# Attention scores of the 128-query units: fp32 products replaced by products of rounded halves, with new tiles and a new order of units

## Chip, cores and metric

The kernel runs on one core of one Trainium2 chip. The metric is device time in microseconds (us) of one execution; three runs of the kernel before are shown. A profile is taken of one further execution.

## What is computed

Causal attention for 4 batches, 12 heads, 448 positions and 64 values a head, and then a feed-forward block on the 1792 tokens of 768 values:

```
scores = q @ k.T / 8, masked above the diagonal
attn   = softmax(scores) ;  a = attn @ v
x      = a, heads side by side: 1792 x 768
xn     = x / sqrt(mean(x*x) + 1e-6) * rms_g
out    = (silu(xn @ w_gate) * (xn @ w_val)) @ w_out
```

The weights have 768 x 1536 (gate, value) and 1536 x 768 elements. All results are fp32.

## The kernel before, in words

**Units.** Attention is cut into units of two heads (a chunk of 128 features, `NP` = 6 chunks) and some queries. Kind 0 has the first 256 queries of a batch against 256 keys, kind 1 the next 128 queries against 384 keys, kind 2 the last 64 queries of two batches at once against 448 keys (`QUERIES`, `KEYS`, line 31). Queries and keys lie transposed, 64 rows a head: head 0 in rows 0 to 63, head 1 in rows 64 to 127. `GROUPS` (line 33) puts the units into three groups of tokens: 512 tokens (two batches of kind 0), 512 (the other two), and 768 (kind 1 of four batches, kind 2 of both pairs). `UNITS` (line 35) lists them by group, then by chunk, then by kind and number; 24 units are of kind 1 and 12 of kind 2. The first 24 units of the list are of kind 0.

**A unit's steps.** `steps_s` (line 173) computes scores on TensorE (`scores`, line 183: for kind 1 one fp32 product a head, 64 rows, 128 weights, 384 columns), then VectorE scales, masks and takes the maximum (line 202), ScalarE takes the exponential with its sum (line 205), VectorE the reciprocal (line 214), GpSimd multiplies (line 210; ScalarE in part of the earlier units). `steps_t` (line 234) transposes the probabilities on TensorE in two halves (a head each, line 249) through the one bank `t`, and VectorE (line 253) or ScalarE (line 255) copies them out. `steps_a` (line 259) multiplies by the values (line 275) and copies the result (line 292).

**Order.** Everything is in program order by hand. The feed-forward block of a group runs while the attention of the next group runs: the main loop (line 900) issues a part of six fp32r products of 128 x 512 (`ffn_part`, lines 475 to 477: each factor is a rounded half plus a rest, three products), then as many attention steps as the pace allows, then one tick. `post(delay, f)` issues f at the end of a later tick. In the group of 768 tokens `round_of_two` (line 809) takes two units at a time in four steps, one a tick: the second transpose of unit p + 1 with a visit (scores of p + 3 and p + 4, value products of p and p + 1), then the transposes of p + 2 (two) and p + 3 (one). Even units use the banks x and y for their scores, odd ones the banks s.

**Loads.** All transfers are issued by SP, in order. `load_qk(p + 4)` (line 151) is posted two ticks after the scores of p into one of four buffers of 2 x 512 elements, whatever the kind; `load_v` (line 160) two ticks after a visit for the next two units, into one of three buffers. Between them stand loads of weights (line 400) and stores of sums of weights (line 454). A transfer into a buffer waits for the last reader of what lay there, and all issues behind it wait with it.

**Splitting into halves.** The kernel splits other operands already: the hidden layer with a ScalarE copy (line 503) and a subtraction on VectorE (line 505) or GpSimd; weights likewise (lines 429, 431).

Of the kernel before, what the change touches and what calls it, by code (L numbers as in the profile page):

```python
# [10 lines left out]
F32 = mybir.dt.float32  # L11
F32R = mybir.dt.float32r
# [10 lines left out]
P = 128  # L23
# [4 lines left out]
W = 512  # L28
# [1 line left out]

QUERIES, KEYS, KB, NKB = (256, 128, 128), (256, 384, 448), (128, 128, 112), (2, 3, 4)

GROUPS = (((0, 2, 0, 0),), ((0, 2, 2, 0),), ((1, 4, 0, 0), (2, 2, 0, W)))
NG = len(GROUPS)
UNITS = [(g, kind, c, k, NP * (first + k) + c, base + QUERIES[kind] * k)
         for g, parts in enumerate(GROUPS) for c in range(NP)
         for kind, n, first, base in parts for k in range(n)]
LAST = {(g, c): max(i for i, u in enumerate(UNITS) if u[0] == g and u[2] == c)
        for g in range(NG) for c in range(NP)}
ENDS = [max(i for i, u in enumerate(UNITS) if u[0] == g) + 1 for g in range(NG)]  # L40
MASKED = -8.0e9


T = dict(c0=0, c1=1, c10=5, c2=4, c20=16, c3=4, c30=18, c26=5, c36=5, c5=6, c50=19, c56=7, exp=1, exp0=3, gt=1, hh=1, hl=4, ws=5, ld2=7,
         ld=4, ld1=11, lv=5, norm0=7, norm1=2, r0=1, acc=10, acc4=7, dg=1, spread=2, r1=5, so=3, wl=2, wl0=7, wl2=5, wl4=1, xl=2, xl0=9)
LOAD = (4, 12, 24, 36, 48, 60, 72, 84)
CONVERT = (14, 26, 38, 50, 62, 85, 86)
# [15 lines left out]
def attention_ffn(ctx: ExitStack, tc: tile.TileContext, qk0, qk1, qk2, v, v2, w, g, out, out2):  # L63
# [35 lines left out]
    def f32(ap):  # L99
        return ap.bitcast(F32)  # L100
# [20 lines left out]
    eps = const.tile([P, 1], F32, name="eps")  # L121
    nc.vector.memset(eps, 1e-6)
    tiny = const.tile([P, 1], F32, name="tiny")
    warm_up = const.tile([P, 1], F32, name="warm_up")
    nc.vector.memset(tiny, 1e-9)
    g_sb = const.tile([P, KD], F32, name="g_sb")

# [4 lines left out]
    def post(delay, fn):  # L132
        if delay <= 0:
            fn()
        else:
            later.setdefault(now[0] + delay, []).append(fn)
# [7 lines left out]
    xr, xh, xl, acc, xq = {}, {}, {}, {}, {}  # L144


    raw_qk, raw_v, hs = {}, {}, {}
    nsc = -1.0 / float(D) ** 0.5
    av_ps = bank("a").rearrange("p (s c) -> p s c", s=2)

    def load_qk(p):
        if p < len(UNITS):
            _, kind, _, _, row, _ = UNITS[p]
            raw_qk[p] = raw.tile([P, 2, W], F32, tag="qk", name="qk_r")
            if kind == 2:
                nc.sync.dma_start(out=raw_qk[p], in_=qk2[row])
            else:
                nc.sync.dma_start(out=raw_qk[p][:, 0], in_=(qk0, qk1)[kind][row])

    def load_v(p):  # L160
        if p < len(UNITS):
            _, kind, _, _, row, _ = UNITS[p]
            raw_v[p] = raw.tile([P, 2, 4, 2, D], F32, tag="v", name="v_r", bufs=3)
            if kind == 2:
                nc.sync.dma_start(out=raw_v[p][: KB[2]], in_=v2[row])
            else:
                nc.sync.dma_start(out=raw_v[p][:, 0, : NKB[kind]], in_=v[row, :, : NKB[kind]])

    def blocks(kind):
# [3 lines left out]
    def steps_s(p):  # L173


        if not 0 <= p < len(UNITS):
            return []
        _, kind, _, _, _, _ = UNITS[p]
        pr = hs[p] = dict(norms=[])
        bl = blocks(kind)  # L180
        nb = 2 * len(bl)

        def scores(pss):
            for i, (o, wd) in enumerate(bl):
                for h in range(1 + (kind == 2)):
                    for e in range(2):
                        r = raw_qk[p][e * D: (e + 1) * D, h]
                        if kind == 2:
                            ps, q0, nq = pss[e][h * D: (h + 1) * D, :wd], 0, D
                        else:  # L190
                            ps, q0, nq = pss[e][:, o: o + wd], i * P, P
                        k0 = nq if kind else 2 * P
                        nc.tensor.matmul(ps, r[:, q0: q0 + nq], r[:, k0: k0 + wd],  # L193
                                         start=True, stop=True)

        def softmax(e, i, pss):
            o, wd = bl[i]
            ps, sp = pss[e][:, o: o + wd], pr["sp"][e][:, o: o + wd]
            n = len(bl) * e + i
            nm, sm, rs = (pr[m][:, n: n + 1] for m in ("nm", "sm", "rs"))  # L200
            mk = mask2 if kind == 2 else mask[:, 3 * P - wd:]
            nc.vector.tensor_tensor_reduce(  # L202
                out=sp, in0=ps, in1=mk, scale=nsc, scalar=3.0e38,
                op0=ALU.add, op1=ALU.min, accum_out=nm)
            post(T["exp" if p >= ENDS[0] else "exp0"], lambda: nc.scalar.activation(  # L205
                sp, sp, AF.Exp, bias=nm, scale=-1.0, accum_out=sm))
            if ENDS[0] - 2 <= p < ENDS[1]:
                pr["norms"].append(lambda: nc.scalar.mul(sp, sp, rs))
            else:
                pr["norms"].append(lambda: nc.gpsimd.tensor_scalar(  # L210
                    sp, sp, rs, 1.0, op0=ALU.mult, op1=ALU.mult))

        def norm():
            nc.vector.reciprocal(pr["rs"][:, :nb], pr["sm"][:, :nb])  # L214
            post(2 if ENDS[0] - 2 <= p < ENDS[0] else 0, lambda: [f() for f in pr["norms"]])

        def step():
            for nm in ("nm", "sm", "rs"):
                pr[nm] = st_p.tile([P, 4], F32, tag=nm, name=nm)
            pr["sp"] = [sp_p.tile([P, S], F32, tag="sp", name="sp") for _ in range(2)]  # L220
            pss = [bank(t_) for t_ in "xy"] if p > ENDS[1] + DP and p % 2 == 0 else [
                bank("s", 2) for _ in range(2)]
            scores(pss)
            for e in range(2):
                for i in range(len(bl)):
                    softmax(e, i, pss)
            post(T["exp" if p >= ENDS[0] else "exp0"], lambda: nc.scalar.activation(
                pr["sm"][:, :nb], pr["sm"][:, :nb], AF.Identity, bias=tiny))
            post(T["norm1" if kind else "norm0"], norm)
            post(2, lambda: load_qk(p + 4))  # L230

        return [step]

    def steps_t(p):

        if not 0 <= p < len(UNITS):
            return []
        _, kind, _, _, _, _ = UNITS[p]
        pr = hs[p]
        kb = KB[kind]  # L240

        def some(e):
            pt = pr["pt", e] = pt_p.tile([P, W], F32, tag=f"pt{e}", name="pt")
            ps = bank("x" if e and p < ENDS[1] + 1 else "t")
            at = 0
            for j in range(NKB[kind]):
                for o, wd in blocks(kind):
                    if kb * j < wd:
                        nc.tensor.transpose(ps[:kb, at: at + P],  # L249
                                            pr["sp"][e][:, o + kb * j: o + kb * (j + 1)], ident)  # L250
                        at += P
            if kind or (e and p < ENDS[0]):
                nc.vector.tensor_copy(pt[:kb, :at], ps[:kb, :at])  # L253
            else:
                nc.scalar.copy(pt[:kb, :at], ps[:kb, :at])

        return [lambda e=e: some(e) for e in (0, 1)]

    def steps_a(p):


        if not 0 <= p < len(UNITS):
            return []
        g_, kind, c, k, _, base = UNITS[p]
        pr = hs[p]
        kb, nq = KB[kind], QUERIES[kind]

        def products():
            for h in range(1 + (kind == 2)):
                at = 0  # L270
                for j in range(NKB[kind]):
                    q0, n = ((0, 2 * P), (P, P))[j] if kind == 0 else (D * h, (P, D)[kind - 1])
                    a0 = at + (D * h if kind == 2 else 0)
                    for e in (0, 1):
                        nc.tensor.matmul(  # L275
                            av_ps[e * D: (e + 1) * D, p % 2, q0: q0 + n], raw_v[p][:kb, h, j, e, :],
                            pr["pt", e][:kb, a0: a0 + n], start=(j == 0), stop=(j == NKB[kind] - 1))
                    at += n if kind == 0 else P

        def copy():  # L280
            if g_ == 2 and base == 0:
                if c < 3:
                    xq[c] = w64_p.tile([P, 2, XT], F32, tag="w64", name="xq")
                xr[g_, c] = xq[c % 3][:, c // 3]
            elif base == 0:
                xr[g_, c] = xr_p.tile([P, W], F32, tag="xr", name="xr")
            x = xr[g_, c][:, base: base + nq]
            if p == ENDS[0] - 2:
                post(1, lambda: nc.scalar.activation(warm_up, eps, AF.Sqrt))
            if p == LAST[g_, c]:  # L290
                post(2, lambda: square(g_, c))
            (nc.scalar.copy if g_ == 1 else nc.vector.tensor_copy)(x, av_ps[:, p % 2, :nq])

        return [products, copy]
# [52 lines left out]

    def rms_first(ps):

        rc = st_p.tile([P, W // P], F32, name="rc", bufs=1)  # L350
        dg = rm_p.tile([P, W], F32, tag="sq", name="dg")
        r = rinv[0] = rm_p.tile([P, W], F32, tag="rms", name="rms", bufs=2)
        nc.scalar.activation(rc, ps, AF.Sqrt, bias=eps, scale=1.0 / DM)
# [703 lines left out]
```

## Time and profile before

| | |
|---|---|
| runs shown | 682.01, 682.80, 683.28 us; median 682.8 |
| the profiled execution | 683.01 us |
| its span, first to last instruction | 681.2 us |
| mean granted clock of TensorE | 1.000 |
| busy: TensorE, weight loads, VectorE, ScalarE, GpSimd | 668.9, 550.4, 533.1, 378.2, 301.0 us |

How to read it: the span is the time between the first and the last instruction in the trace; what the execution takes beyond it (1.8 us) lies before and after. PE is the matrix engine TensorE, PEld its weight loads (which can run beside products), DVE is VectorE, ACT ScalarE, POOL GpSimd, SP the engine that issues the transfers. L193 is line 193 of the kernel. The busy time of PE is modelled from its starts; an fp32 product appears as two records. Waits name the engine and line that ended them.

### The profile page before, as it was taken

The page shows a single profiled execution, that of the slowest core. Times are in us where ns is not written, and L with a number is a line of the kernel's source. Part 1 is how long each engine was busy: PE and PEld are TensorE (multiplying, and loading weights), DVE is VectorE, ACT ScalarE, POOL GpSimd, SP SyncE. Part 2 cuts the span into 40 slices and gives each one's busy share as a digit, 9 for nine tenths or more (in the row PEclk, how much of TensorE's full clock was granted, in tenths as well). Part 3 has the DMA queues.
Part 4 walks back from the last instruction along what each step waited for, and adds up shares of the span by engine and source line. Part 5 has one row for each costly group of instructions (what it writes and reads, how often), then busy time and mean ns, then how long its engine had stood idle before and what let it go on. Part 6 is the DMA issues. An engine that isn't in the chain of part 4 may idle for free. (4 is left out here: it accounts for less than half of the span.)

```text
span 681.2 us, 11945 instructions
## 1 busy us (share of the span) xinstructions
PE 668.9 (98%) x4122; PEld 550.4 (81%) x4122; DVE 533.1 (78%) x1053; ACT 378.2 (56%) x855; POOL 301.0 (44%) x268
## 2 busy tenths in 40 slices
PE   9989999999999999999999999999999999999997
PEld 6566877777777777777777777888999999999997
DVE  4998998999888486777777877387576777779993
ACT  6986779797876444545545453444524342455550
POOL 4971121222235427565765666563353645302220
PEclk9999999999999999999999999999999999999999
DMA  7765788787877456767666645316657474553641
GB/s 256 255 234 199 217 242 298 233 259 233 284 270 279 159 163 228 220 237 211 226 224 222 210 160 179 123 62 206 207 182 252 164 270 172 190 164 83 176 139 63
DMA packets 71357, 138.82 MB, mean 204 GB/s; under 512 B 7744, under 2 KB 39232, under 8 KB 71296
## 3 DMA queue, kind: packets, MB, share of 16 engines
q1 hardware_dynamic: 71296, 138.05, 62.7%
q8 instruction: 33, 0.54, 0.3%
q14 instruction: 28, 0.23, 0.1%
HBM read 104.21 MB, written 33.82 MB: 203 GB/s over the span
## 5 line engine op out<-in xcount | busy, mean ns | idle before, releaser
L210 POOL TENSOR_SCALAR sp<-sp,rs 128x384 f32<-128x384 f32 (+2 forms) x112 | 78.6, 719 | 90.8 <-DVE rs L214 80.3
L475 PE MATMUL m_ps<-xh,w_h 128*128 128x512 f32 x276 | 117.4, 425 | 0.0
L205 ACT ACTIVATE sp<-sp,nm 128x384 f32<-128x384 f32 (+3 forms) x168 | 87.2, 521 | 42.3 <-DVE nm L202 42.3
L477 PE MATMUL m_ps<-xh,w_l 128*128 128x512 f32 x276 | 108.3, 392 | 0.0
L476 PE MATMUL m_ps<-xl,w_h 128*128 128x512 f32 x276 | 108.2, 392 | 0.0
L415 POOL TENSOR_SCALAR w<-w 128x768 f32<-128x768 f32 x36 | 39.2, 1090 | 103.3 <-ACT w_c L414 97.7
L103 POOL TENSOR_TENSOR a_l<-w_q,a_h 128x768 fp32r<-128x768 f32 x24 | 49.5, 2066 | 52.5 <-ACT a_h L516 50.7
L275 PEld LDWEIGHTS a_ps<-pt,v_r 128*64 128x64 f32 (+1 forms) x864 | 41.8, 137 | 31.3 <-issue 9.2
L275 PE MATMUL a_ps<-pt,v_r 128*64 128x128 f32 (+2 forms) x864 | 59.5, 268 | 4.2 <-DVE pt L253 2.8
L103 POOL TENSOR_TENSOR w_l<-w_r,w_h 128x768 fp32r<-128x768 f32 x30 | 59.5, 1991 | 6.2 <-ACT w_h L429 6.0
L477 PEld LDWEIGHTS m_ps<-xh,w_l 128*128 128x128 f32 x276 | 51.9, 188 | 12.0
L475 PEld LDWEIGHTS m_ps<-xh,w_h 128*128 128x128 f32 x276 | 51.9, 188 | 11.8 <-issue 3.7
L253 DVE COPY pt<-t_ps 128x384 f32<-128x384 f32 (+1 forms) x71 | 42.4, 597 | 23.9 <-PE t_ps L249 23.5
L202 DVE CUSTOM_DVE_ANT_0 sp<-s_ps,mask 128x128 f32<-128x128 f32 (+3 forms) x136 | 49.8, 414 | 12.1 <-PE s_ps L193 11.1
L475 PE MATMUL m_ps<-hh,w_h 128*128 128x512 f32 x144 | 58.6, 407 | 0.0
L476 PEld LDWEIGHTS m_ps<-xl,w_h 128*128 128x128 f32 x276 | 52.2, 189 | 7.6
L477 PE MATMUL m_ps<-hh,w_l 128*128 128x512 f32 x144 | 56.2, 391 | 0.0
L476 PE MATMUL m_ps<-hl,w_h 128*128 128x512 f32 x144 | 56.2, 390 | 0.0
L249 PE MATMUL t_ps<-ident,sp 128*128 128x128 f32 (+1 forms) x309 | 50.1, 275 | 0.1
L249 PEld LDWEIGHTS t_ps<-ident,sp 128*128 128x128 f32 (+1 forms) x309 | 37.8, 137 | 14.4 <-issue 2.0
L193 PE MATMUL s_ps<-qk_r 64*128 64x128 f32 (+3 forms) x296 | 42.4, 423 | 0.5 <-DVE nm L202 0.4
L516 ACT CAST a_h<-w_q 128x768 fp32r<-128x768 f32 (+1 forms) x48 | 35.0, 754 | 13.5 <-DMA w_q<-wz 4.2
(196 smaller groups left out, 1677.5 us busy)
## 6 DMA issues: line engine op xcount, KB each, us to landing
w<-in_w SPq DMA_DIRECT2D x36, 768.0 KB, 5.4
w<-w_c SPq DMA_DIRECT2D x36, 384.0 KB, 5.9
w_r<-w SPq DMA_DIRECT2D x36, 384.0 KB, 4.9
qk_r<-in_qk SPq DMA_DIRECT2D x48, 256.0 KB, 4.3
qk_r<-in_qk SPq DMA_DIRECT2D x12, 512.0 KB, 5.6
v_r<-in_v SPq DMA_DIRECT2D x12, 448.0 KB, 4.8
v_r<-in_v SPq DMA_DIRECT2D x24, 192.0 KB, 3.4
wy<-w_r SPq DMA_DIRECT2D x24, 192.0 KB, 4.1
```

The lines of the kernel that those rows point to most:

```text
L103: nc.gpsimd.tensor_tensor(out_, a, b, op=op)
L193: nc.tensor.matmul(ps, r[:, q0: q0 + nq], r[:, k0: k0 + wd], start=True, stop=True)
L202: nc.vector.tensor_tensor_reduce(out=sp, in0=ps, in1=mk, scale=nsc, scalar=3.0e38, op0=ALU.add, op1=ALU.min, accum_out=nm)
L205: post(T["exp" if p >= ENDS[0] else "exp0"], lambda: nc.scalar.activation(sp, sp, AF.Exp, bias=nm, scale=-1.0, accum_out=sm))
L210: pr["norms"].append(lambda: nc.gpsimd.tensor_scalar(sp, sp, rs, 1.0, op0=ALU.mult, op1=ALU.mult))
L249: nc.tensor.transpose(ps[:kb, at: at + P], pr["sp"][e][:, o + kb * j: o + kb * (j + 1)], ident)
L253: nc.vector.tensor_copy(pt[:kb, :at], ps[:kb, :at])
L275: nc.tensor.matmul(av_ps[e * D: (e + 1) * D, p % 2, q0: q0 + n], raw_v[p][:kb, h, j, e, :], pr["pt", e][:kb, a0: a0 + n], start=(j == 0), ...
L415: (T["c1" if s > 4 else "c10"], lambda: nc.gpsimd.tensor_scalar(hf_, hf_, 0.0, 1.0, op0=ALU.mult, op1=ALU.mult)),
L475: nc.tensor.matmul(ps, wh[:, k, :], mh, start=(first and k == ks[0]), stop=False)
L476: nc.tensor.matmul(ps, wh[:, k, :], ml, start=False, stop=False)
L477: nc.tensor.matmul(ps, wl[:, k, :], mh, start=False, stop=(last and k == 5))
```

## The change

Units of kind 1 get their queries and keys split into a rounded half h (fp32r, ScalarE) and the rest l (VectorE), and their scores become h·h + l·h + h·l, each an fp32r product accumulated in the same bank, the two heads in turn. The split of unit p + 3 is posted in the step of p: 2 ticks later, or 6 for even p in the last group (`qh`, `qh1`), and the subtraction one tick behind the copy. The order within a chunk of the last group becomes kind 1, 1, 2, 1, 1, 2. Query and key tiles of kinds 0 and 1 shrink to 512 elements (four buffers), kind 2 has one buffer of its own, and its load is posted two units ahead instead of four; the values of kind 2 have one buffer of their own, the other kinds three smaller ones. Of the two transposed blocks of a kind-1 unit the first is copied out by ScalarE instead of VectorE. A small tile (`rc`) moves to another pool.

```diff
-GROUPS = (((0, 2, 0, 0),), ((0, 2, 2, 0),), ((1, 4, 0, 0), (2, 2, 0, W)))
+GROUPS = (((0, 0, 0), (0, 1, 0)), ((0, 0, 2), (0, 1, 2)),
+          ((1, 0, 0), (1, 1, 0), (2, 0, 0), (1, 2, 0), (1, 3, 0), (2, 1, 0)))
...
-UNITS = [(g, kind, c, k, NP * (first + k) + c, base + QUERIES[kind] * k)
-         for g, parts in enumerate(GROUPS) for c in range(NP)
-         for kind, n, first, base in parts for k in range(n)]
+UNITS = [(g, kind, c, k, NP * (first + k) + c, QUERIES[kind] * k + W * (kind == 2))
+         for g, parts in enumerate(GROUPS) for c in range(NP) for kind, k, first in parts]
...
-T = dict(c0=0, ...
+T = dict(qh=2, qh1=6, ql=1, c0=0, ...
...
     def load_qk(p):
         if p < len(UNITS):
             _, kind, _, _, row, _ = UNITS[p]
-            raw_qk[p] = raw.tile([P, 2, W], F32, tag="qk", name="qk_r")
-            if kind == 2:
-                nc.sync.dma_start(out=raw_qk[p], in_=qk2[row])
-            else:
-                nc.sync.dma_start(out=raw_qk[p][:, 0], in_=(qk0, qk1)[kind][row])
+            two = kind == 2
+            raw_qk[p] = raw.tile([P, 1 + two, W], F32, tag=f"qk{two}", name="qk_r", bufs=1 if two else 4)
+            nc.sync.dma_start(out=raw_qk[p], in_=qk2[row] if two else (qk0, qk1)[kind][row])
+
+    def split_qk(p):
+        x = raw_qk[p][:, 0]
+        h, l = halves[p] = [raw.tile([P, W], F32R, tag=n, name=n, bufs=2) for n in ("qh", "ql")]
+        nc.scalar.copy(h, x)
+        post(T["ql"], lambda: nc.vector.tensor_tensor(l, x, f32(h), op=ALU.subtract))
...
-            raw_v[p] = raw.tile([P, 2, 4, 2, D], F32, tag="v", name="v_r", bufs=3)
             if kind == 2:
+                raw_v[p] = raw.tile([P, 2, 4, 2, D], F32, tag="v2", name="v_r", bufs=1)
                 nc.sync.dma_start(out=raw_v[p][: KB[2]], in_=v2[row])
             else:
+                raw_v[p] = raw.tile([P, 1, 3, 2, D], F32, tag="v", name="v_r", bufs=3)
                 nc.sync.dma_start(out=raw_v[p][:, 0, : NKB[kind]], in_=v[row, :, : NKB[kind]])
...
         def scores(pss):
+            if kind == 1:
+                for n, (a, b) in enumerate(((0, 0), (1, 0), (0, 1))):
+                    for e in range(2):
+                        x, y = (halves[p][j][e * D: (e + 1) * D] for j in (a, b))
+                        nc.tensor.matmul(pss[e][:, : KEYS[1]], x[:, : P], y[:, P:],
+                                         start=n == 0, stop=n == 2)
+                return
...
-            post(2, lambda: load_qk(p + 4))
+            if p + 3 < len(UNITS) and UNITS[p + 3][1] == 1:
+                post(T["qh1"] if p > ENDS[1] and p % 2 == 0 else T["qh"], lambda: split_qk(p + 3))
+            for n in (2, 4):
+                if p + n < len(UNITS) and (UNITS[p + n][1] == 2) == (n == 2):
+                    post(2, lambda n=n: load_qk(p + n))
...
-            if kind or (e and p < ENDS[0]):
+            if kind == 2 or (kind and e) or (e and p < ENDS[0]):
                 nc.vector.tensor_copy(pt[:kb, :at], ps[:kb, :at])
```

## Rows read from the trace of the kernel before

**Rows 1.** The page: busy time by engine, granted clock in 40 slices.

```profile
PE 668.9 (98%) x4122; PEld 550.4 (81%) x4122; DVE 533.1 (78%) x1053; ACT 378.2 (56%) x855; POOL 301.0 (44%) x268
...
PEclk9999999999999999999999999999999999999999
```

**Rows 2.** Windows: length; busy (count) of PE, PEld, DVE, ACT, POOL; clock; DMA.

```profile
236.00:413.00 177.00, 176.92 (x1393) 131.35 (x1391) 136.13 (x340) 85.35 (x215) 110.38 (x105) 1.00 0.64 205
```

**Rows 3.** Waits of TensorE's matmuls, 236 to 430 us: total, times, longest.

```profile
PE a_ps L275 <- DVE pt L253: 0.5, 1, 0.5
```

**Rows 4.** Timeline of TensorE, second unit of a visit: start, duration, what, count.

```profile
293.76 0.48 PE L193 MATMUL x_ps<-qk_r 64*128 64x384 f32 x1
293.76 0.48 PE L193 MATMUL y_ps<-qk_r 64*128 64x384 f32 x1
294.08 0.48 PE L193 MATMUL x_ps<-qk_r 64*128 64x384 f32 x1
```

**Rows 5.** Timeline of TensorE, a kind-1 unit between two changes of shape.

```profile
250.08 0.59 PE L193 MATMUL x_ps<-qk_r 64*128 64x384 f32 x1
...
250.51 0.48 PE L193 MATMUL x_ps<-qk_r 64*128 64x384 f32 x1
...
250.93 0.55 PE L275 MATMUL a_ps<-pt,v_r 128*64 128x128 f32 x6
```

**Rows 6.** The chain that ended last: nine fp32r products of 384 columns.

```profile
583.55 1.56 PE s_ps L625 x9
```

**Rows 7.** Timeline of the weight loads in the visit of rows 4.

```profile
293.44 0.19 PEld L193 LDWEIGHTS x_ps<-qk_r 64*128 64x128 f32 x1
```

**Rows 8.** Groups by form: busy, mean ns, idle before; nearest copies and subtractions.

```profile
L503 ACT CAST hh<-t_sb 128x512 fp32r<-128x512 f32 x24 | 14.8, 615 | 20.4 <-DVE t_sb L502 20.4
...
L505 DVE TENSOR_TENSOR hl<-t_sb,hh 128x512 fp32r<-128x512 f32 x12 | 8.6, 714 | 0.3 <-ACT hh L503 0.3
...
L253 DVE COPY pt<-t_ps 128x384 f32<-128x384 f32 x47 | 25.9, 551 | 17.5 <-PE t_ps L249 17.2
...
L255 ACT COPY pt<-t_ps 128x384 f32<-128x384 f32 x24 | 11.2, 467 | 3.3 <-PE t_ps L249 3.3
```

**Rows 9.** Timeline of TensorE: starts of visits and their parts.

```profile
261.40 2.08 PE L275 MATMUL a_ps<-pt,v_r 112*64 112x64 f32 x64
...
270.11 0.49 PE L249 MATMUL t_ps<-ident,sp 128*128 128x128 f32 x3
...
280.44 0.52 PE L249 MATMUL t_ps<-ident,sp 128*128 128x128 f32 x3
280.88 0.98 PE L193 MATMUL s_ps<-qk_r 64*64 64x448 f32 x8
281.80 0.59 PE L193 MATMUL x_ps<-qk_r 64*128 64x384 f32 x1
...
282.64 1.53 PE L275 MATMUL a_ps<-pt,v_r 128*64 128x128 f32 x24
```

**Rows 10.** Timelines of TensorE and GpSimd after the visit at 270 us.

```profile
276.96 0.49 PE L249 MATMUL t_ps<-ident,sp 128*128 128x128 f32 x3
278.67 0.49 PE L249 MATMUL t_ps<-ident,sp 128*128 128x128 f32 x3
...
276.50 2.78 POOL L210 TENSOR_SCALAR sp<-sp,rs 128x384 f32<-128x384 f32 x4 [2.94 <-DVE rs L214]
```

**Rows 11.** Timeline of ScalarE after the same visit; idle before in brackets.

```profile
277.88 0.63 ACT L493 ACTIVATE t_sb<-gr 128x512 f32<-128x512 f32 x1 [2.43 <-DVE gr L492]
```

**Rows 12.** SP's queue, then times to landing: all of line 156, and 252.68.

```profile
243.35 8.81 SPq L165 DMA_DIRECT2D v_r<-in_v  x2
...
252.68 0.42 SPq L156 DMA_DIRECT2D qk_r<-in_qk  x1
...
DMA to landing us min/median/max: 3.9/5.6/8.2
...
DMA to landing us min/median/max: 7.1/7.1/7.1
```

More of the change, by code (lines that the diff above doesn't have):

```diff
@@ L41 @@
 MASKED = -8.0e9
-T = dict(c0=0, c1=1, c10=5, c2=4, c20=16, c3=4, c30=18, c26=5, c36=5, c5=6, c50=19, c56=7, exp=1, exp0=3, gt=1, hh=1, hl=4, ws=5, ld2=7,
+T = dict(qh=2, qh1=6, ql=1, c0=0, c1=1, c10=5, c2=4, c20=16, c3=4, c30=18, c26=5, c36=5, c5=6, c50=19, c56=7, exp=1, exp0=3, gt=1, hh=1, hl=4, ws=5, ld2=7,
          ld=4, ld1=11, lv=5, norm0=7, norm1=2, r0=1, acc=10, acc4=7, dg=1, spread=2, r1=5, so=3, wl=2, wl0=7, wl2=5, wl4=1, xl=2, xl0=9)
@@ L123, in attention_ffn @@
     tiny = const.tile([P, 1], F32, name="tiny")
-    warm_up = const.tile([P, 1], F32, name="warm_up")
+    rc = const.tile([P, W // P], F32, name="rc")
     nc.vector.memset(tiny, 1e-9)
@@ L144, in attention_ffn @@
     xr, xh, xl, acc, xq = {}, {}, {}, {}, {}
-    raw_qk, raw_v, hs = {}, {}, {}
+    raw_qk, raw_v, hs, halves = {}, {}, {}, {}
     nsc = -1.0 / float(D) ** 0.5
@@ L288, in copy @@
             if p == ENDS[0] - 2:
-                post(1, lambda: nc.scalar.activation(warm_up, eps, AF.Sqrt))
+                post(1, lambda: nc.scalar.activation(rc[:, :1], eps, AF.Sqrt))
             if p == LAST[g_, c]:
@@ L348, in rms_first @@
     def rms_first(ps):
-        rc = st_p.tile([P, W // P], F32, name="rc", bufs=1)
         dg = rm_p.tile([P, W], F32, tag="sq", name="dg")
```

## The prediction

> **What bounds the kernel now.** I read the page of the profile first. TensorE is busy 98% of the span and its granted clock is full in all 40 slices [rows 1], so the level is 2.4 GHz throughout and no slice is a candidate for a clock effect. Next the windows: the units with 128 queries are scored between about 236 and 413 us (the first three a little before), in the group of 768 tokens. In these 177 us TensorE is busy 176.9, VectorE 136, ScalarE 85, GpSimd 110 [rows 2]. Since "busy" of TensorE is modelled, I checked it with the waits: over 236 to 430 us the matmul queue shows one wait, of 0.5 us [rows 3]. So in this stretch an instruction of TensorE that becomes shorter shortens the run, as long as nothing else arrives late, and after it the chain that ends last is again mostly matmuls, with every transfer placed relative to them. The forecast is therefore a sum over TensorE, and the rest of the work is to look for what may come late.
>
> **What one unit's scores cost today.** The timeline of a visit that scores two such units one after the other shows the anatomy [rows 4]. Each fp32 product is recorded twice, so a unit (two heads) has four records, and the list of units has 24 of this kind; the two heads start within 0.01 us of each other, in the two halves of the rows, and run side by side. From 293.76 to 294.08 one pass takes 0.32 us; a unit has two, 0.64 us. Around the passes lie two gaps that belong to the change of tile shape: the first matmuls of a block take 0.59 against 0.48 us, that is 0.105 us of weight load in the open, and after the last pass (250.51 + 0.32 = 250.83) the next product starts only at 250.93, 0.10 us later [rows 5].
>
> **What they will cost.** A unit becomes three products of fp32r halves for each head, again in pairs of row halves, so three steps. The trace has no fp32r product with 64 rows. The nearest row is the fp32r product with 128 rows and the same 384 columns in the later stage: nine of them in 1.56 us, 0.173 us each [rows 6]. Two half-height products side by side should be such a product, so I take 3 x 0.173 = 0.52 us for the unit. The load in the open and the gap at the end stay, as the tile shape is the same. The saving is 0.64 - 0.52 = 0.12 us a unit, 24 x 0.12 = **2.9 us**. Bounds: at best a step costs half a pass of today, 0.16 us, and 24 x (0.64 - 0.48) gives 3.8 us less. At worst the heads don't run side by side in this type: 6 x 0.173 = 1.04, 24 x 0.40 = 9.6 us more. I stand near the good end because today's pairs of the same shape do run side by side [rows 4].
>
> Weights are loaded 6 times a unit instead of 4. Today a load lies under the pass before it: in the visit above the second unit's loads begin at 293.44, while the first unit's second pass (293.44 to 293.76) still runs in the same row halves, and the second unit starts with no load in the open [rows 7]. A load in the open cost 0.105 us; a step of 0.173 us covers that, so I count nothing. If this cover fails, two further loads a unit are open.
> The Trainium skill, "TensorE: Matmul & The Clock Gate", section "Part 3: Packing small matmuls — row/col tiling", says that a weight load overlaps matmuls in flight only when its row group differs from theirs; by that sentence the loads of the second and third product would all be in the open, the change would lose, and the trace disagrees, with loads at 293.44 under a pass of their own row halves.
>
> **Splitting.** Each of the 24 units gains a ScalarE copy 128x512 to fp32r and a VectorE subtraction of that shape. The nearest rows are the same operations on the hidden layer: 0.615 and 0.714 us [rows 8]. One of two transposed blocks of each unit goes from VectorE (0.551 us) to ScalarE (0.467 us). ScalarE gains 24 x (0.615 + 0.467) = 26 us, VectorE 24 x (0.714 - 0.551) = 3.9 us. Laid on the 177 us, ScalarE rises from 85 to 111, VectorE from 136 to 140: neither becomes the bound. Their place matters more. Copy, subtraction and scores of a unit stand one tick apart, some 2.6 us (a visit is four ticks and takes 10.3 us, 270.11 to 280.44 [rows 9]), and the copy waits for a load issued four ticks before it. The transposed block must leave its bank before the next transposes, 1.7 us later (276.96 to 278.67 [rows 10]); after the visit at 270 us ScalarE stands idle for 2.43 us up to 277.88 [rows 11], and that is where the copy falls. The normalisation on GpSimd starts at 276.50; its first two blocks are done by 277.9 and their transpose comes at 278.67 [rows 10], 0.8 us of slack that the moved copy does not shorten. I count nothing for all of this; without the cover the price is at most one such copy, 0.5 us, on some of 24 units.
>
> **Order and loads.** The order of a chunk becomes 1, 1, 2, 1, 1, 2 (kinds) instead of 1, 1, 1, 1, 2, 2. TensorE does the same transposes and value products; scoring visits with two units of kind 1 go from five to six, worth 0.1 us, left out. The loads are what moves. SP takes its queue in order and today stands most of the time at the value loads, which wait for value products (8.81 us at 243.35) [rows 12]. With separate value buffers the waits for kind 1 vanish, since the buffer was last used four or five units before, and stores and weight loads queued behind move up, which costs nothing. Kind 2 gets one buffer each for queries with keys and for values. Its query load is now posted two units ahead instead of four, and in every other case (six of twelve) it stands behind a value load that waits for a kind-2 product of the same visit. I price that case: transposes 0.44 (280.44 to 280.88), kind-2 scores 0.92 (to 281.80), kind-1 scores 0.84 (to 282.64) less the 0.12 saved, one kind-2 product block 2.08 / 2 = 1.04 [rows 9] make 3.1 us after the visit's start; two issues of 0.42 come first, so the load goes out at 4.0. In the same sequence today (252.68) it lands after 7.1 us [rows 12], at 11.1. It is needed in the next visit, which starts 10.3 us later, after transposes and one unit of 0.72 us, at 11.5. So 0.4 us remain. With the slowest landing of the twelve, 8.2 us [rows 12], it is 0.7 us late. I take zero, and for the bound six loads late by 0.7, 4.2 us.
>
> **Sum.** The profiled execution took 683.01 us, span 681.2 and 1.8 around it. 683.01 - 2.9 = 680.1; the median of the runs shown is 0.2 lower than that execution, so 679.9. A measurement of this kernel can tell about 0.2% (1.4 us) from no change, and 2.9 us is 0.4%.
>
> **Rivals.**
> 1. Late data takes the gain back: query loads of kind 2, or a rounded half that VectorE delivers late. For it: 0.4 us of slack in six visits and SP's order. Against it: SP waits less, ScalarE and VectorE idle in the right places. Half of the bound, 2.1 us, back gives 682.0; all of it 684.1. Chance 0.17.
> 2. Slower, by open weight loads: with three short steps a load could be held until the matmul in its own rows ends. Two more open loads a unit are 24 x 2 x 0.105 = 5.0 us, and one more in the second unit of each of six double visits, 0.6 us; less the 2.9 saved, 2.7 us slower, 685.5. It decides from 2.9 / 54 = 0.054 us a load in the open. Against it: the loads at 293.44. Chance 0.08. By the Trainium skill's rule named above, this would be the outcome.
> 3. The heads run one after the other in fp32r: plus 9.6, 692.4. Against it: the pairs of today. Chance 0.07. Then the change doesn't do what it says.
>
> **How the numbers follow.** The forecast case has the remaining 0.68: 679.9, itself between 679.0 (0.16 us a step) and about 681.3, where the gain is no longer told from nothing. Rival 1 falls about no change, the other two are slower: faster 0.68, same 0.16, slower 0.16. The range takes the forecast and rival 1 whole, with the scatter of the runs (682.0 to 683.3, 0.7 either side) at the low end: 678.3 to 684.1; left out are rivals 2 and 3, 0.15.
>
> **What would show it.** Right: in a double visit the pairs of fp32r products stand 0.17 us apart, the heads within 0.01 us, and the visit is some 0.24 us shorter; ScalarE near 111 us in the stretch; no wait of TensorE over a few tenths. Rival 1: waits of the score products for the query load or the subtracted half. Rival 2: each pair's matmuls longer by 0.1 us and the steps 0.28 apart. Rival 3: six starts 0.17 apart. I would be wrong altogether if the stretch from 236 us shortened while the end did not move, a later stage waiting for something that did not come earlier.

## The result and the profile after

The changed kernel takes 692.05 us (median, 690.94 to 693.95) against 682.78 us: ratio 1.0141, 95% interval 1.0128 to 1.0153. The forecast was 679.9. It is slower by 9.3 us, close to what rival 3 gave, but not by rival 3's mechanism: the products do what the forecast said. Its profiled execution took 693.95 us, the slowest of the four, with a span of 691.9 us. Of a later run (683.08 us, section 3 of the experiments) one execution of ten, at 696.92 us, stands apart from the rest and is left out of the ratio.

The page of the changed kernel, and its windows (columns as in [rows 2]):

```profile
PE 668.8 (97%) x4170; PEld 556.0 (80%) x4170; DVE 544.2 (79%) x1053; ACT 401.4 (58%) x903; POOL 306.8 (44%) x268
...
236.00:413.00 177.00, 168.79 (x1354) 129.29 (x1352) 138.69 (x318) 100.94 (x245) 110.15 (x98) 0.98 0.61 204
```

TensorE does the same busy time in a span 10.7 us longer. In the 177 us that were full before [rows 2] it is now idle for 8.2 us, and its granted clock is 0.98. The square sum that opens the second group's feed-forward block and the column sums that follow attention bracket the stretch; their first starts are, before and after (one line each, then the other kernel's):

```profile
L372 PE MATMUL x_ps<-acc,ones x2: 592/594/595, 233.4 to 233.8; 128*128 128x512 f32 x2
L536 PE MATMUL t_ps<-ones,acc x12: 164/250/250, 429.6 to 430.7; 128*128 128x1 f32 x12
...
L387 PE MATMUL x_ps<-acc,ones x2: 592/594/595, 234.5 to 234.9; 128*128 128x512 f32 x2
L551 PE MATMUL t_ps<-ones,acc x12: 165/250/250, 440.3 to 441.4; 128*128 128x1 f32 x12
```

From the one to the other it was 196.2 us and is 205.8: 9.6 of the 10.7 us arise here, 1.1 before, nothing after.

**The products** are as forecast. The timeline of TensorE in a visit, kind 1 first, then kind 2:

```profile
297.50 0.44 PE L193 MATMUL s_ps<-qh 64*128 64x384 f32 x2
297.78 0.34 PE L193 MATMUL s_ps<-qh,ql 64*128 64x384 f32 x2
297.96 0.33 PE L193 MATMUL s_ps<-ql,qh 64*128 64x384 f32 x2
298.22 0.59 PE L205 MATMUL x_ps<-qk_r 64*64 64x448 f32 x1
```

The two heads run side by side (x2 in one row), the second and third step start 0.18 us apart with their weight loads under the step before (the first step is 0.10 us longer, the open load at the start of a block, as before [rows 5]), and the unit takes 298.22 - 297.50 = 0.72 us where it took 0.84 (281.80 to 282.64, [rows 9]). Rivals 2 and 3 are out.

**The waits** are new. TensorE's matmul queue, 236 to 430 us (total, times, longest), where there was one wait of 0.5 us [rows 3]:

```profile
PE t_ps L265 <- ACT pt L271: 4.6, 5, 1.9
PE t_ps L265 <- DVE pt L269: 1.9, 1, 1.9
PE x_ps L193 <- DVE ql L162: 1.4, 1, 1.4
PE a_ps L291 <- DVE pt L269: 0.5, 1, 0.5
PE s_ps L193 <- DVE ql L162: 0.2, 1, 0.2
```

Of 8.6 us, 6.5 are transposes that find their one bank not copied out, by ScalarE or VectorE, and 1.6 are scores waiting for the rest l. No score product waits for a query load, so rival 1's loads are out too; its other half, the late rest, is there but small.

**What stands behind them** shows at 270 us. VectorE, then GpSimd, then TensorE, in the changed kernel:

```profile
270.46 4.00 DVE L162 TENSOR_TENSOR ql<-qk_r,qh 128x512 fp32r<-128x512 f32 x2
...
268.27 1.85 POOL L103 TENSOR_TENSOR w_l<-w_r,w_h 128x768 fp32r<-128x768 f32 x1
270.08 1.62 POOL L103 TENSOR_TENSOR hl<-t_sb,hh 128x512 fp32r<-128x512 f32 x1
271.66 2.26 POOL L103 TENSOR_TENSOR w_l<-w_r,w_h 128x768 fp32r<-128x768 f32 x1
...
274.52 0.53 PE L193 MATMUL x_ps<-qh,ql 64*128 64x384 f32 x1 [1.43 <-DVE ql L162]
```

Two subtractions that I priced at 0.71 us each take 4.00 us together: GpSimd runs two-operand operations without a break from 268.27 to 273.92, and the second subtraction ends at 274.46, 0.54 us after the last of them, while TensorE stands. Another place in the same kernel, VectorE and then GpSimd:

```profile
349.13 0.68 DVE L162 TENSOR_TENSOR ql<-qk_r,qh 128x512 fp32r<-128x512 f32 x1
...
347.31 3.51 POOL L222 TENSOR_SCALAR sp<-sp,rs 128x384 f32<-128x384 f32 x4 [2.35 <-DVE rs L226]
...
348.43 1.83 POOL L222 TENSOR_SCALAR sp<-sp,rs 128x384 f32<-128x384 f32 x1
```

Beside the normalisation, which has one tensor operand, the subtraction takes 0.68 us; but the four normalisations take 3.51 us where four took 2.78 [rows 10]. The one in the last row begins before the subtraction and takes 1.83 us. Over the stretch to 413 us I set each subtraction against GpSimd's TENSOR_TENSOR rows: the eight that meet none take 0.67 to 0.69 us; of the twelve that meet one, ten take about 1.0 to 2.3. The other two began 0.17 us before GpSimd's operation and take 0.68, and then GpSimd's takes 1.38 or 1.39 us instead of 1.0. Both cases in a row, each time VectorE and then GpSimd:

```profile
337.43 1.12 DVE L162 TENSOR_TENSOR ql<-qk_r,qh 128x512 fp32r<-128x512 f32 x1
336.99 1.01 POOL L103 TENSOR_TENSOR acc<-acc,sq 128x384 f32<-128x384 f32 x1 [0.35 <-ACT sq L324]
...
338.47 0.68 DVE L162 TENSOR_TENSOR ql<-qk_r,qh 128x512 fp32r<-128x512 f32 x1
338.64 1.39 POOL L103 TENSOR_TENSOR acc<-acc,sq 128x384 f32<-128x384 f32 x1 [0.64 <-ACT sq L324]
```

The group (last row: its minimum, median and maximum over the whole span, in ns):

```profile
L162 DVE TENSOR_TENSOR ql<-qk_r,qh 128x512 fp32r<-128x512 f32 x20 | 20.9, 1058 | 0.0
...
L162 DVE TENSOR_TENSOR ql<-qk_r,qh x24: 672/689/2297, 174.3 to 411.1; 128x512 fp32r<-128x512 f32 x24
```

The Trainium skill, "SBUF — State Buffer", section "SBUF: two separate sides", says that a VectorE operation with two SBUF inputs and a GpSimd operation that reads SBUF exclude each other for the length of a whole instruction, whichever comes first. The rows of two-operand operations agree: a subtraction that comes second ends 0.54 us after GpSimd's last operation, and one that comes first leaves GpSimd's the longer. The normalisation agrees only in part: the one that began at 348.43 did not hold up the subtraction at 349.13, and was itself the longer one.

**The clock** adds to it. Windows of 4 us in the changed kernel (the column before the last two is the granted clock):

```profile
272.00:276.00 4.00, 2.40 (x18) 1.51 (x18) 4.00 (x7) 0.62 (x1) 1.92 (x1) 0.84 0.26 98
276.00:280.00 4.00, 4.00 (x32) 3.36 (x29) 2.86 (x11) 3.61 (x11) 0.00 (x0) 0.73 0.00 2
360.00:364.00 4.00, 2.40 (x13) 1.65 (x11) 4.00 (x4) 0.23 (x1) 3.02 (x2) 1.00 0.95 360
364.00:368.00 4.00, 3.68 (x58) 2.58 (x60) 3.08 (x10) 1.61 (x6) 0.00 (x0) 1.00 0.80 305
376.00:380.00 4.00, 3.08 (x17) 2.35 (x19) 2.11 (x7) 2.52 (x5) 3.98 (x3) 0.64 1.01 338
380.00:384.00 4.00, 4.00 (x37) 3.42 (x36) 2.85 (x9) 3.10 (x11) 0.00 (x0) 0.93 0.34 129
```

After TensorE stood for 1.43 us (to 274.52) and for 1.87 us (to 376.92) it ran at the 1.2 GHz level for a while; after the 1.9 us up to 364.3 it did not. The lost shares, (0.16 + 0.27 + 0.36 + 0.07) x 4 us, are 3.4 us. The sum: waits 8.6 - 0.5, clock 3.4, products -2.9 give 8.6 of the 9.6 us. This sum is of the slowest execution. One of the four had a mean clock of 1.000 and took 690.94 us, so 8.2 us of loss are there without the clock.

### The profile page after: what moved, and what is told of

Same layout as the page of the kernel before. It is cut to its first block, busy times and chain, and to the rows that moved or that the text cites. A ratio compares the mean times of both kernels' runs of the same rounds, so it can differ in the third digit from the quotient of the medians.

```text
span 691.9 us, 12120 instructions
## 1 busy us (share of the span) xinstructions
PE 668.8 (97%) x4170; PEld 556.0 (80%) x4170; DVE 544.2 (79%) x1053; ACT 401.4 (58%) x903; POOL 306.8 (44%) x268
## 5 line engine op out<-in xcount | busy, mean ns | idle before, releaser
L222 POOL TENSOR_SCALAR sp<-sp,rs 128x384 f32<-128x384 f32 (+2 forms) x112 | 82.2, 751 | 90.9 <-DVE rs L226 78.2
L217 ACT ACTIVATE sp<-sp,nm 128x384 f32<-128x384 f32 (+2 forms) x168 | 87.2, 521 | 41.4 <-DVE nm L214 41.3
L430 POOL TENSOR_SCALAR w<-w 128x768 f32<-128x768 f32 x36 | 37.8, 1051 | 103.8 <-ACT w_c L429 98.3
L291 PEld LDWEIGHTS a_ps<-pt,v_r 128*64 128x64 f32 (+1 forms) x864 | 43.4, 140 | 29.5 <-issue 8.2
L214 DVE CUSTOM_DVE_ANT_0 sp<-s_ps,mask 128x128 f32<-128x128 f32 (+3 forms) x136 | 49.9, 415 | 10.7 <-PE s_ps L205 9.3
L269 DVE COPY pt<-t_ps 112x512 f32<-112x512 f32 (+1 forms) x47 | 29.1, 619 | 18.6 <-PE t_ps L265 18.5
L446 DVE TENSOR_TENSOR w_l<-w_c,w_h 128x768 fp32r<-128x768 f32 x36 | 37.8, 1049 | 3.3 <-ACT w_h L444 3.3
```

The source lines that it names most:

```text
L214: nc.vector.tensor_tensor_reduce(out=sp, in0=ps, in1=mk, scale=nsc, scalar=3.0e38, op0=ALU.add, op1=ALU.min, accum_out=nm)
L222: pr["norms"].append(lambda: nc.gpsimd.tensor_scalar(sp, sp, rs, 1.0, op0=ALU.mult, op1=ALU.mult))
L291: nc.tensor.matmul(av_ps[e * D: (e + 1) * D, p % 2, q0: q0 + n], raw_v[p][:kb, h, j, e, :], pr["pt", e][:kb, a0: a0 + n], start=(j == 0), ...
L430: (T["c1" if s > 4 else "c10"], lambda: nc.gpsimd.tensor_scalar(hf_, hf_, 0.0, 1.0, op0=ALU.mult, op1=ALU.mult)),
L446: post(T[("wl0", "wl0", "wl2", "wl2", "wl4")[s] if s < 5 else "wl"], lambda: nc.vector.tensor_tensor(l, t, f32(h), op=ALU.subtract))
```

## The experiments

All ratios are to the kernel before, on the same chip. Line numbers are those of the changed kernel.

**1. Which part: order, subtraction, moved copy, products.**

Order and buffers alone (fp32 scores, no splits, both blocks copied by VectorE):

```diff
-            if kind == 1:
+            if False:
...
-            if p + 3 < len(UNITS) and UNITS[p + 3][1] == 1:
+            if p + 3 < len(UNITS) and UNITS[p + 3][1] == 9:
...
-            if kind == 2 or (kind and e) or (e and p < ENDS[0]):
+            if kind or (e and p < ENDS[0]):
```

> The change without the halves: new order and new tiles and buffers, fp32 scores, both transposed blocks copied by VectorE as before. Theory A (VectorE: the subtraction, stretched beside GpSimd, makes the copies out of the bank of the transposes late): as before, 682.8, at most 1 us off. Theory B (ScalarE: the moved copy stands behind squares that wait for GpSimd): as before too. Theory C (order and buffers: loads late, or the chunk's sums in new places): about 690.

Measured: 683.04 us, ratio 0.9997 (0.9985 to 1.0009). Order, buffers and moved loads cost nothing; theory C falls.

No subtraction:

```diff
-        post(T["ql"], lambda: nc.vector.tensor_tensor(l, x, f32(h), op=ALU.subtract))
+        halves[p] = [h, h]
```

> The change without the subtraction on VectorE: the rest l is left out and the three products all use the rounded half h; copy, order, tiles and moved copy stay. Theory A: 680 to 682, the gain of the products appears, no wait of the transposes over 0.5 us on VectorE. Theory B: the waits on ScalarE's copy (4.6 us in the changed kernel) stay, 687 to 690. Theory C: 690.

Measured: 683.99 us, 1.0015 (1.0003 to 1.0028), 2 us above theory A's range and 3 below theory B's. The subtraction carries 8 of the 9.3 us; 2.4 us of waits for ScalarE's copy remain:

```profile
PE t_ps L265 <- ACT pt L271: 2.4, 5, 1.5
```

Both blocks on VectorE (the last hunk of the first diff alone):

> The change with both transposed blocks copied by VectorE as before. Theory A: no better than the changed kernel, 691 to 695, VectorE has 13 us more to do and the waits move to its copies. Theory B: 685 to 688, the waits on ScalarE's copy are gone. Theory C: 692.

Measured: 691.81 us, 1.0119 (1.0087 to 1.0151), as theory A said. With the subtraction in place the copy is late on either engine.

Splits made, fp32 scores (the first hunk of the first diff alone):

> The change with the splits still made but the scores computed as fp32 products from the unsplit tile. Products cheaper by 0.12 us a unit, as forecast: 2 to 3 us slower than the changed kernel, 694, less up to 1.6 us for the waits on the rest l that fall away. If the fp32r products themselves were the loss: 683.

Measured: 695.07 us, 1.0157 (1.0133 to 1.0181). The products are not the loss; that they are a gain is seen here in the medians, 3 us, while the intervals overlap.

No subtraction and both blocks on VectorE:

> The change without the subtraction (l left out, three products of h) and with both transposed blocks copied by VectorE as before. If the moved copy on ScalarE makes the 4 us between the run without the subtraction (684.0) and the forecast: 680.0 to 681. If something else of the change makes them (the ScalarE split copy, the loads): 683 to 685.

Measured: 681.65 us, 0.9981 (0.9968 to 0.9993); its profiled execution has a span of 678.4 us, and the stretch is 193.8 us instead of 196.2:

```profile
L387 PE MATMUL x_ps<-acc,ones x2: 592/594/595, 233.0 to 233.4; 128*128 128x512 f32 x2
L551 PE MATMUL t_ps<-ones,acc x12: 164/250/250, 426.8 to 427.9; 128*128 128x1 f32 x12
```

Without subtraction and moved copy most of the forecast's 2.9 us appears in the stretch, 2.4 us, but only 1.3 us in the runs. The two parts do not add: taking the moved copy back is worth 2.3 us without the subtraction and 0.2 us with it.

**2. Collision or amount.** Squares and their sums of the last group left out (`if b == 2 and c: return` at the head of `square`):

> The change without the squares of the last five chunks of the last group (ScalarE) and their sums (GpSimd): left out. If the copies on ScalarE are late because they stand behind squares that wait for GpSimd, and if those sums are what the subtraction collides with: 684 to 688. If the subtraction is slow beside the weights' and hidden layer's GpSimd work instead: 690 to 692.

Measured: 695.43 us, 1.0189 (1.0147 to 1.0230), slower than the change. Squares that wait for GpSimd do hold ScalarE's copy at some places: the two waits that stand behind one in the changed kernel (0.75 us up to 308.44, 1.87 us up to 376.92; the second is shown in section 3) are gone here. But another, where ScalarE waits for VectorE, grows from 1.25 to 3.15 us, and the subtractions are longer (their median is 1.01 us here, and 0.69 in the changed kernel). So taking the squares out alone gains nothing, and this run does not rule them out as a cause of the late copies.

GpSimd's two-operand subtractions of the second feed-forward block left out (`l = h`, `hl = hh` there):

> The change, unaltered in attention, without GpSimd's two-operand subtractions in the feed-forward block that runs beside it (the rests of 24 weights and 12 hidden tiles of the second group are left out, the rounded halves stand in their place). If the loss is the collision of VectorE's subtraction with GpSimd's two-operand operations: 680 to 683, the subtraction's mean under 0.75 us. If it is the amount of work or its place on VectorE alone: 688 to 691, the mean may fall but the waits of the transposes stay.

Measured: 686.88 us, 1.0055 (1.0038 to 1.0071): between the two. The mean falls to 0.87 us, since the sums of squares still collide, and 5 us of the loss go. All that TensorE still waits for in the stretch is ScalarE's copy, 4.4 us. As some subtractions still collide, and GpSimd has less work altogether, the run doesn't say what collision costs as a whole.

The subtraction in other places. Two ticks earlier:

```diff
-T = dict(qh=2, qh1=6, ql=1,
+T = dict(qh=0, qh1=4, ql=1,
```

> The change with both splits two ticks earlier (copy in the visit itself, ahead of the exponentials, subtraction one tick later), where GpSimd waits for the reciprocals and VectorE has no copy out of the transposes' bank behind it. If place and collision with GpSimd make the loss: 683 to 686, the subtraction's mean falls from 1.06 us to under 0.8. If the amount of work on VectorE makes it: 690 to 693. If the copy ahead of the exponentials delays the normalisation: waits of the transposes for GpSimd, over 690.

Measured: 690.60 us, 1.0107 (1.0090 to 1.0124), with the subtraction and the longest waits of TensorE:

```profile
L162 DVE TENSOR_TENSOR ql<-qk_r,qh x24: 629/684/2316, 170.0 to 404.0; 128x512 fp32r<-128x512 f32 x24
...
PE t_ps L265 <- ACT pt L271: 5.8, 6, 2.0
```

A miss for the collision theory, and a telling one: 23 of the 24 subtractions take 0.63 to 0.69 us and only one collides, and still just 1.5 us of the loss go. TensorE now waits for ScalarE's copy, and four of the six waits (5.3 of the 5.8 us) stand behind squares that waited 2.9 to 3.6 us for GpSimd's sums.

Right behind the reciprocals, so beside the normalisation (`qh=1, qh1=5, ql=1`, both blocks on VectorE), and with the copy first (`qh=0, qh1=4, ql=2`):

> Copy one tick earlier, subtraction right behind the reciprocals in VectorE's order, so that it runs beside GpSimd's normalisation (one operand, no collision seen); both transposed blocks copied by VectorE. Collision theory: mean of the subtraction under 0.8 us, 682 to 686. If the place makes the copies late: 687 to 691.

> As the last, with the ScalarE copy in the visit itself, ahead of the exponentials, so that the subtraction never waits for it. Collision theory: 682 to 685. If the copy delays the exponentials and so the normalisation: 686 to 690.

Measured: 687.15 us, 1.0066 (1.0051 to 1.0081), and 686.55 us, 1.0058 (1.0043 to 1.0073). The subtraction in the first of these and the normalisation on GpSimd, there and in the run with order and buffers alone:

```profile
L162 DVE TENSOR_TENSOR ql<-qk_r,qh x24: 666/673/693, 172.8 to 401.0; 128x512 fp32r<-128x512 f32 x24
...
L222 POOL TENSOR_SCALAR sp<-sp,rs 128x384 f32<-128x384 f32 x44 | 37.6, 870 | 33.7 <-DVE rs L226 33.7
...
L222 POOL TENSOR_SCALAR sp<-sp,rs 128x384 f32<-128x384 f32 x44 | 30.9, 720 | 39.1 <-DVE rs L226 39.1
```

Every subtraction is short now, 4.7 us of the loss with VectorE's copies (691.81 to 687.15) are gone, and the clock stays full. Part of the 4.7 is the clock: the run with VectorE's copies took 689.9 and 690.0 us at a mean clock of 0.999, and 693.6 and 693.7 us at 0.994 and 0.997. In exchange each normalisation is 0.15 us longer, and VectorE's other two-operand work still collides. The subtraction made twice in this place:

```diff
-        post(T["ql"], lambda: nc.vector.tensor_tensor(l, x, f32(h), op=ALU.subtract))
+        for _ in (0, 1):
+            post(T["ql"], lambda: nc.vector.tensor_tensor(l, x, f32(h), op=ALU.subtract))
```

> The run with the subtraction behind the reciprocals and both blocks copied by VectorE (687.15), with every subtraction made twice: 24 more operations of 0.68 us, none beside a two-operand operation of GpSimd. If a subtraction that does not collide still costs by its length, as 681.65 to 687.15 suggests (0.23 us of 0.68 each): 692 to 696, since the queue has less room. If the first was the whole trouble and length is free: 687 to 688.

Measured: 701.26 us, 1.0264 (1.0247 to 1.0282). Its waits of TensorE, and its subtraction and normalisation:

```profile
PE t_ps L266 <- POOL sp L223: 7.4, 6, 2.3
PE t_ps L266 <- DVE pt L270: 6.1, 10, 1.2
...
L163 DVE TENSOR_TENSOR ql<-qk_r,qh x48: 664/692/1016, 172.6 to 415.0; 128x512 fp32r<-128x512 f32 x48
...
L223 POOL TENSOR_SCALAR sp<-sp,rs 128x384 f32<-128x384 f32 x44 | 42.4, 977 | 37.1 <-DVE rs L227 37.1
```

24 more subtractions cost 14.1 us, 0.59 us each; the first 24 cost 5.5 us (681.65 to 687.15). None meets a two-operand operation of GpSimd, but they are not undisturbed: 20 of the 48 take 0.87 to 1.02 us beside the normalisations, which grow in turn. Half of the waits are late copies on VectorE, half normalisations that GpSimd ends later. So more work on VectorE costs here without two-operand collisions too; how much by its length and how much by what it does to the normalisation, this run doesn't separate.

**3. The copy's place.** The subtraction behind the reciprocals, the first block on ScalarE as in the change:

> As the run with the subtraction behind the reciprocals, with the first transposed block copied by ScalarE as in the change. Collision theory: 682 to 686, VectorE less loaded, some waits for ScalarE's copy left.

Measured: 689.21 us, 1.0100 (1.0077 to 1.0122), with 5.7 us of waits for ScalarE's copy, up to 2.3 us each, four of the six behind squares that waited for GpSimd's sums. In the changed kernel such waits end where a visit begins. ScalarE there, and TensorE:

```profile
375.37 0.52 ACT L324 ACTIVATE sq<-xq 128x384 f32<-128x384 f32 x1 [2.43 <-POOL acc L103]
375.80 0.60 ACT L518 CAST hh<-t_sb 128x512 fp32r<-128x512 f32 x1
376.31 0.47 ACT L271 COPY pt<-t_ps 128x384 f32<-128x384 f32 x1
...
376.92 0.69 PE L265 MATMUL t_ps<-ident,sp 128*128 128x128 f32 x3 [1.87 <-ACT pt L271]
```

The copy of the odd unit's block stands behind a hidden-layer copy, and both stand behind a square that waited 2.43 us for GpSimd's sum of squares; the next transposes follow right behind it. The sum is late in part through the subtractions beside it: the two here take 2.46 us, and the sum 1.44 us instead of 1.0. So ScalarE keeps the copy for even units alone:

```diff
-            if kind == 2 or (kind and e) or (e and p < ENDS[0]):
+            if kind == 2 or (kind and (e or p % 2)) or (e and p < ENDS[0]):
```

> Subtraction behind the reciprocals; ScalarE copies the first block only of even kind-1 units, whose transposes stand right behind a visit, VectorE that of odd ones, after whose transposes the next visit follows. If ScalarE's copy is late only there (all five of its waits in the changed kernel are at the start of a visit): 682.5 to 685, no wait for ScalarE's copy over 0.4 us after 236 us. If VectorE's remaining work is late anyway: 686 to 688, as with all copies on VectorE.

> As the last, with ScalarE's split copy in the visit itself. 682 to 685; if the split copy ahead of the exponentials costs, 1 us more than the last.

> The change as it is, with that rule for the copies alone. Collisions remain: 687 to 690, between the change and the last two. If ScalarE's copies were a small part: 691.

Measured: 683.08 us, 1.0006 (0.9994 to 1.0018), with `qh=1, qh1=5, ql=1`; 682.47 us, 1.0002 (0.9987 to 1.0018), with `qh=0, qh1=4, ql=2`; and 696.12 us, 1.0196 (1.0180 to 1.0212), with the change's own places. TensorE's waits in the first, and the largest group of the third:

```profile
PE t_ps L265 <- DVE rs L226: 0.6, 1, 0.6
PE a_ps L291 <- DVE pt L269: 0.5, 1, 0.5
PE t_ps L265 <- DVE pt L269: 0.2, 1, 0.2
PE t_ps L265 <- ACT pt L271: 0.2, 1, 0.2
...
PE t_ps L265 <- DVE pt L269: 9.0, 5, 4.2
```

In the first the waits are 1.5 us instead of 8.6, and the first two runs are back at the time before. Neither rule does it alone. The third is a miss: with colliding subtractions the new copy rule is worse than the change, for the copy that VectorE took back now stands behind them (the wait of 4.2 us ends behind two of 1.77 and 2.28 us). In the second the stretch is 195.0 us, 1.2 us shorter than before, but one wait of 1.1 us for VectorE at 485 us, not there before, gives that back.

**4. The subtraction on GpSimd.** With the early split, in its idle time before the normalisation, with VectorE's copies, with the new copy rule, and for odd units alone:

> The early split with the subtraction on GpSimd, in its idle time before the normalisation, and both transposed blocks copied by VectorE as before. If VectorE's subtraction and ScalarE's moved copy are the whole loss: 680 to 682, faster than before. If GpSimd's normalisation comes late: waits of the transposes for it, 685 to 690.

> Early split, subtraction on GpSimd in its idle time before the normalisation, ScalarE's copy for even units alone. VectorE then has less to do than before the change. If VectorE's lateness was all that was left: 680 to 682, faster than before. If GpSimd's 33 us more, or its two-operand subtraction meeting VectorE's other operations, make new lateness: 683 to 686.

> Early split, the subtraction of odd units on GpSimd before the normalisation, of even units on VectorE behind the reciprocals, ScalarE's copy for even units alone. 680 to 682.5 if the load is only to be spread; 683 to 685 if GpSimd's share of it makes new collisions.

Measured: 686.65 us, 1.0049 (1.0034 to 1.0065); 686.61 us, 1.0057 (1.0043 to 1.0070); 686.08 us, 1.0055 (1.0041 to 1.0068). The last two are above the ranges given. On GpSimd it is another two-operand operation, of 1.35 us; that VectorE's own then meet it is the likely reason, which no run here separates. No version is clearly faster than the kernel before.

## Why the prediction was wrong

- **The bound** was right: TensorE was full in the stretch, and what makes it wait shows in full at the end.
- **The products** were right: 0.72 us a unit where 0.84 less 0.12 was forecast; weight loads hidden, heads side by side.
- **Order and loads** were right: the run with these alone gives 0.9997, and no product waited for a query load.
- **Splitting is the step that failed**: "I count nothing for all of this; without the cover the price is at most one such copy, 0.5 us, on some of 24 units." The subtraction was priced at 0.714 us from the group of [rows 8]. That group belongs to the first feed-forward block, where GpSimd's two-operand operations fill 11.6 us from 60 to 236 us, against 65.6 us from 236 to 413. In the stretch that matters it meets those for weights, hidden layer and squares, and takes 1.06 us in the mean and 2.3 at most. VectorE's busy time rose by 11.1 us, where the forecast had 3.9. Nor was 0.7 us at that place free: VectorE has idle time in total (136 of 177 us), but the forecast did not ask how much of it lies ahead of the copy that must free the transposes' bank. Measured: 8 us for the subtraction as placed. Moving it to the normalisation, where it is short, gave back 2.8 us with ScalarE's copies as in the change, 4.7 us with VectorE's, and 13.0 us with ScalarE's for even units alone (696.12 to 683.08). So its price depends on where the copies stand, and no one figure is the collision's.
- **The moved copy**, also counted at nothing, is worth 2.3 us in the run without the subtraction. I judged it by one idle stretch of ScalarE [rows 11] after an even unit's transposes; the waits come at the odd unit's, where the copy stands behind hidden-layer copies and squares, and a square can wait for GpSimd. Without the subtraction that is 2.4 us of waits, with it 4.6 us. Taken together, the change (692.05), the subtraction moved (689.21), the copy rule alone (696.12) and both (683.08) show the two terms acting on each other, which a sum of terms priced one by one does not hold.
- **Rival 1** named the late rest but bounded only the loads, 4.2 us; a chain of copies waiting for one bank was not in it, nor the 3.4 us of clock that follow the waits in the profiled execution.
- The trace of before could have shown it. Its VectorE sums of weights have the same two-operand form (minimum, median, maximum in ns):

```profile
L450 DVE TENSOR_TENSOR w_r<-w_r x48: 541/549/2162, 242.6 to 425.8; 128x384 f32<-128x384 f32 x48
```

A median of 0.55 us with a maximum of 2.16 in this very stretch is the bound that the forecast lacked.

What stays open: how the 8 us split between collision, length, the delay of the normalisation and of the sums of squares, and clock, since the runs differ in more than one of these; why even the best version does not bring the forecast's 2.9 us; and the wait at 485 us in some versions, which was not followed up.

## What to carry to other kernels

Where one engine is full, price an added operation on another engine at its place, not by that engine's total idle time: ask which single-buffered bank its queue must free next and how much slack is there. Take the duration from rows of the same stretch with minimum, median and maximum, and look at what GpSimd runs beside it: a VectorE operation with two SBUF operands (128 x 512) here took 0.68 us alone and up to 2.3 us beside a two-operand GpSimd operation. If such work must go in, put it where GpSimd has one-operand work and give each copy out of a shared bank to the engine whose queue is short at that tick; both together brought back 9 us here, and one of them alone made the kernel 4 us slower.

## What the runs showed of the hardware that was not expected

- Two fp32r products of 64 rows in different row halves run side by side, 0.18 us a step for 384 columns, hardly more than the 0.173 us of a product of 128 rows [rows 6].
- VectorE and GpSimd hold each other up both ways: a subtraction that comes second ends 0.54 us after GpSimd's last two-operand operation, one that comes first takes 0.68 us and GpSimd's operation 1.39 instead of 1.0, and beside the subtraction the normalisation grows from 0.72 to 0.87 us, and to 0.98 us with two, and the second subtraction to 1.0.
- Waits of TensorE of 1.4 and 1.9 us were followed by stretches at the 1.2 GHz level, in this execution 3.4 us of lost work; another of 1.9 us was not.
